# Loading q and k in longer rows, with the queries ordered by residue mod 8, in an attention and feed-forward kernel

## The chip, the core and the metric

The kernel runs on one core of one Trainium2 chip. A core has TensorE (PE: matmuls; its weight loads are listed apart as PEld), VectorE (DVE), ScalarE (ACT), GpSimd (POOL) and SyncE (SP, which here only issues transfers), and 16 DMA engines between HBM and the on-chip memory SBUF. TensorE writes into PSUM. The metric is the time of one execution on the device, in microseconds (us). Three runs of the kernel before took 181.08, 181.47 and 181.53 us, median 181.47.

## The reference

Two parts follow one another. The first is attention with 4 batches, 8 heads, 768 tokens and 64 numbers for each head. A query sees the 96 last tokens (itself included) and the first 8 tokens of the sequence, with a bias that grows linearly with distance. The second is a feed-forward layer on 3,072 tokens of width 512, inner width 1,024.

```python
scores = np.matmul(q, k.transpose(0, 1, 3, 2)) / np.sqrt(D)
is_global = pos[None, :] < n_global                      # 8
is_local = (rel >= 0) & (rel < n_local)                  # 96
keep = is_global | is_local
dist = np.where(is_global & ~is_local, float(n_local), np.abs(rel))
scores = np.where(keep, scores - slopes[:, None, None] * dist[None], -1e9)
a = softmax(scores)
x = np.matmul(a, v)            # then heads side by side: [3072, 512]

h = x @ w_in                   # [3072, 1024]
solu = h * softmax(h)
ln = (solu - mean) / np.sqrt(var + 1e-6) * g_ln
out = ln @ w_out               # [3072, 512]
```

Inputs and output are float32.

## The kernel before

The work is cut into 12 units: one unit is a batch and a third of its tokens (256 queries), for all 8 heads, numbered 0 to 11. What is done for a unit is a set of short steps, and a long string `ORDER` says in which order the steps are written into the program. Every engine and every queue works through its own instructions in just that order; waits between engines follow from the data. A step's name is followed by what it needs: an engine or queue (S for SP, A for ACT, D for DVE, P for POOL), the unit, and a head pair or a half.

```python
ORDER = """
gb id off:1 cap off:0 g:A dist:1 mask:1:0 dist:0 q:S:0 cq:A:0 tq:0 eq:A:0 zero k:S:0 ck:D:0 tk:0
ek:A:0 S:0:3 gk:0 mask:1:6 X:0:3 S:0:0 X:0:0 gS:0 mask:0:7 gX:0 v:A:0:0 mask:1:7 mask:0:2 mask:0:6
q:S:1 cq:D:1 k:S:1 mask:0:5 mask:0:1 S:0:1 S:0:2 X:0:1 tq:1 eq:A:1 ck:P:1 selV tk:1 ek:D:1 S:1:0
k:S:3 X:0:2 mask:0:3 ck:D:3 tk:3 q:S:2 v:S:0:1 ek:A:3 gk:1 fill cq:D:2 cv:D:0 gv0:0 q:S:4 q:S:3
... (cut)
o:A:9:1 d:S:10:1 O:10:1 o:A:10:1 Q:11:0:1 t:11:0:0 e:D:11:0:0 t:11:0:1 e:D:11:0:1 st:S:7 t:11:1:0
e:D:11:1:0 t:11:1:1 e:A:11:1:1 O:11:0:0 O:11:0:1 st:S:10 O:11:1:0 O:11:1:1 st:S:9 Z:P:11:0:1
o:D:11:0:0 o:D:11:0:1 st:S:11:0:1 Q:11:1:0 Q:11:1:1 Z:P:11:1:1 o:A:11:1:1 o:D:11:1:0 st:S:11:0:0
st:S:11:1:0 st:A:11:1:1
"""
```

The names: `q`, `k`, `v` load; `cq`, `ck`, `cv` cast to fp16; `tq`, `tk` turn q or k (64 numbers of a head onto partitions) on TensorE and `eq`, `ek` bring the result from PSUM to SBUF; `dq` turns q with a DMA transpose instead. `S` makes the scores of a head pair, `X` their exponentials, `M` multiplies them with the mask; `gS`, `gX` the same for the 8 global tokens; `L` the sums of the softmax, `I` their inverse, `V` the values, `N` the normalized result. For each half of a unit (128 tokens) `A` is the first product of the feed-forward layer, `E` its exponential, `U` the product of the two, `Q` its squares, `Z` the statistics, `d` a DMA transpose (`t` and `e` on TensorE for the last unit), `O` the second product, `o` its scaling, `st` the store. `wi`, `wo`, `g`, `sc`, `pr`, `sm`, `mean`, `ce`, `cm` load and prepare the weights. `warm:n` issues n matmuls on zeros.

The loads, the casts and the turning of q and k:

```python
    def staged(shape, name):
        return stage.tile(shape, FP32, name=name, tag="in32", bufs=NIN)

    def load_qk(queue, name, u):
        b, s = units[u]
        t = held[name + "32", u] = staged([P, H, 2 * D], name + "32")
        queues[queue].dma_start(
            out=t,
            in_=(q if name == "q" else k)[b, :, ts(s, UQ)].rearrange("h (p r) d -> p h (r d)", r=2),
        )

    def load_v(queue, u, j):
        b, s = units[u]
        if ("v32", u) not in held:
            held["v32", u] = staged([P, H, 2, D], "v32")
        queues[queue].dma_start(
            out=held["v32", u][:, :, j], in_=v[b, :, ts(2 * s + j, P)].rearrange("h p d -> p h d")
        )

... (cut)

    def warm_up(n):

        t = small([P, 512], FP32, "warm")
        for _ in range(n):
            nc.tensor.matmul(out=t, lhsT=held["zeros"][:, 0:P], rhs=held["zeros"],
                             start=True, stop=True)

... (cut)

    def cast_qk(engine, name, u):
        t = held[name + "16", u] = attn.tile([P, 2, H, D], FP16, name=name + "16")
        cast(engine, t, held.pop((name + "32", u)).rearrange("p h (r d) -> p r h d", r=2))

... (cut)

    def turn(name, u):
        src = held.pop((name + "16", u))
        t = held["p" + name, u] = small([P, 2, NPAIR, P], FP16, name + "turned")
        for r in range(2):
            for g in range(NPAIR):
                nc.tensor.transpose(
                    out=t[:, r, g, :],
                    in_=src[:, r, 2 * g : 2 * g + 2].rearrange("p h d -> p (h d)"),
                    identity=held["ident"],
                )

    def evac_q(engine, u):
        t = held["qT", u] = attn.tile([P, 2, NPAIR, QC], FP16, name="qT")
        cast(engine, t, held.pop(("pq", u)))

    def evac_k(engine, u):
        t = held["kT", u] = attn.tile([P, NPAIR, UQ], FP16, name="kT", bufs=4)
        cast(engine, t.rearrange("p g (i r) -> p g i r", r=2),
             held.pop(("pk", u)).rearrange("p r g i -> p g i r"))

    def turn_q_dma(queue, u):
        t = held["qT", u] = attn.tile([P, 2, NPAIR, QC], FP16, name="qT")
        queues[queue].dma_start_transpose(
            out=t.rearrange("p r g i -> p (r g) i"),
            in_=held.pop(("q16", u)).rearrange("p r h d -> p (r h d)"),
        )
```

In HBM a head's tokens lie one after another, 64 float32 numbers (256 bytes) each. `load_qk` puts tokens 2p and 2p+1 of all 8 heads on partition p: 128 partitions, 8 heads, runs of 512 bytes. The queries are then ordered with the even tokens first and the odd ones behind (r is 0 or 1), and so are the columns of scores, sums and values. Scores and norm read and write them like this:

```python
    def scores(u, g):
        s = units[u][1]
        qT = held["qT", u]
        sc = held["sc", u, g] = big("sc")
        for j, a, e, o in blocks(s)[0]:
            for m in range(2):
                r = slice(m * D, m * D + D)
                nc.tensor.matmul(
                    out=sc[:, m, o : o + e - a].rearrange("p (r i) -> p r i", r=2),
                    lhsT=held["kT", u - s + j // 2][r, g, ts(j % 2, P)],
                    rhs=qT[r, :, g, a // 2 : e // 2], start=True, stop=True,
                )

... (cut: expo, keep, the global tokens, sums, invert, values)

    def norm(u):
        xT = held["xT", u] = attn.tile([P, NPAIR, UQ], FP16, name="xT", bufs=3)
        nc.vector.tensor_tensor(
            out=xT, in0=held.pop(("pa", u)).rearrange("p g r i -> p g (r i)"),
            in1=held.pop(("rlb", u)), op=ALU.mult,
        )

... (cut: the feed-forward steps)

    def ff_turn_dma(queue, t):
        held["uT", t] = msb.tile([P, NFC, P], FP16, name="uT", bufs=3)
        queues[queue].dma_start_transpose(out=held["uT", t], in_=held["un", t])

... (cut)

    def store(queue, u, r=None, h=None):
        b, s = units[u]
        rows = out[ds(b * S + s * UQ, UQ), :].rearrange("(p r) c -> p r c", r=2)
        sl = slice(0, 2) if r is None else slice(r, r + 1)
        c = part(h, D_MODEL)
        queues[queue].dma_start(out=rows[:, sl, c], in_=held["osb", u][:, sl, c])
```

The store writes pairs of tokens again (r=2), 4 KB for each partition.

## Time and profile before

The profile is of one execution with a span of 182.2 us.

| | before |
|---|---|
| median of three runs | 181.47 us |
| span of the profiled execution | 182.2 us |
| mean granted TensorE clock | 0.981 of full |
| HBM read, written | 23.07 MB, 6.29 MB |
| loads of q, and of k | 12 of 512 KB each, median 6.6 and 7.1 us from issue to landing |
| loads of v | 24 of 256 KB |
| DMA transposes | 9 of q, 22 in the feed-forward layer |
| turning on TensorE (k: 96 matmuls, q: 24) | 9.5 and 3.1 us busy |

How to read it: a busy share is taken over the whole span. The page also cuts the span into 40 equal slices and gives the busy share of each in tenths (9 is 90% or more), for the engines and for the mean of the 16 DMA engines, and what they moved in GB/s. A list of waits says which engine, at which instruction, waited for which releaser: us in total, times, the longest. A stretch of time can be asked for by itself: then each engine's busy us (and instructions), the granted clock, the DMA share and GB/s follow. A packet is one contiguous piece that a DMA engine moves.

### The profile page before, as it was taken

Reading aid. Unit: us, or ns where it says so; the run is one execution under the profiler, and the core shown is the slowest. Engines: PE = TensorE matmul, PEld = TensorE weight load, DVE = VectorE, ACT = ScalarE, POOL = GpSimd, SP = SyncE. Lnnn points to the kernel's source line nnn. Section 1 sums busy time; section 2 is a strip of 40 time slices with the busy share of each in tenths; the row PEclk is TensorE's granted clock in tenths of the full one; section 3 lists DMA queues with packets and bytes.
Section 4 is the critical chain, followed back from the end, with each engine's and each line's share of the span. In section 5 each row is a group of like instructions: output and inputs, shape, how many; then the busy total and the mean of one; then the engine's idle time right before and its main releaser. Section 6 shows DMA issues by size and latency. Waiting matters only on the chain. (4 is left out here: it accounts for less than half of the span.)

```text
span 182.2 us, 3846 instructions
## 1 busy us (share of the span) xinstructions
PE 151.0 (83%) x1456; PEld 81.2 (45%) x1456; DVE 114.4 (63%) x180; ACT 144.1 (79%) x232; POOL 85.1 (47%) x188
## 2 busy tenths in 40 slices
PE   0474538995699499889999999999999999998880
...
DMA  5999999999899949799999999999979942068062
GB/s 117 279 290 252 271 205 177 280 306 243 191 294 234 159 114 167 150 258 155 200 294 290 147 157 274 182 251 277 281 93 323 246 89 58 4 140 262 13 242 90
DMA packets 87506, 36.69 MB, mean 201 GB/s; under 512 B 59456, under 2 KB 84544, under 8 KB 87488
## 3 DMA queue, kind: packets, MB, share of 16 engines
q1 hardware_dynamic: 83680, 34.74, 87.9%
q0 software_dynamic: 544, 1.05, 3.3%
...
q14 instruction: 7, 0.06, 0.1%
HBM read 23.07 MB, written 6.29 MB: 161 GB/s over the span
## 5 line engine op out<-in xcount | busy, mean ns | idle before, releaser
L344 ACT ACTIVATE pt<-sc 128x896 f16<-128x896 f32 (+1 forms) x48 | 40.0, 864 | 9.6 <-PE sc L335 9.3
L459 PE MATMUL ph<-w_in,xT 128*128 128x512 f16 x192 | 44.9, 380 | 1.2 <-DVE xT L444 0.7
L535 PE MATMUL po<-gw,uT 128*128 128x512 f16 x192 | 44.6, 379 | 0.3 <-DVE osb L547 0.2
L481 DVE SCALAR_TENSOR_TENSOR un<-e,ph 128x1024 f16<-128x1024 f16 (+1 forms) x26 | 29.2, 1135 | 15.9 <-ACT e L473 7.0
L351 DVE TENSOR_TENSOR pt<-pt,mask 128x896 f16<-128x896 f16 (+1 forms) x48 | 31.5, 685 | 4.4 <-ACT pt L344 4.3
L473 ACT ACTIVATE e<-ph 128x1024 f16<-128x1024 f32 (+1 forms) x26 | 24.8, 954 | 5.5 <-PE ph L459 4.8
L535 PEld LDWEIGHTS <-uT 128*128 128x128 f16 x192 | 18.2, 98 | 22.1 <-issue 0.7
L490 ACT ACTIVATE sq<-un 128x1024 f16<-128x1024 f16 (+1 forms) x26 | 25.7, 988 | 2.8 <-DVE un L481 2.6
L459 PEld LDWEIGHTS <-xT 128*128 128x128 f16 x192 | 17.5, 98 | 23.1 <-DVE xT L444 1.7
L444 DVE TENSOR_TENSOR xT<-pa,rlb 128x1024 f16<-128x1024 f32 x12 | 14.6, 1220 | 20.0 <-ACT rlb L416 16.8
L335 PE MATMUL sc<-qT,kT 64*128 64x128 f16 (+2 forms) x256 | 17.8, 260 | 5.6 <-ACT qT L135 2.5
L139 POOL CAST v<-v 128x1024 f16<-128x1024 f32 x9 | 9.7, 1084 | 20.7 <-DMA v<-in_v_dram 20.6
L335 PEld LDWEIGHTS <-kT 64*128 64x128 f16 x256 | 9.8, 105 | 14.2 <-issue 10.2
L510 POOL TENSOR_SCALAR w<-s,w 128x1 f32<-128x1 f32 x22 | 7.6, 344 | 17.6 <-ACT sq L490 11.9
L137 DVE COPY kT<-kturned 128x1024 f16<-128x1024 f16 x10 | 12.2, 1219 | 4.7 <-PE kturned L300 4.7
L398 PE MATMUL lb<-pt,ones 128*64 128x128 f16 (+2 forms) x256 | 11.3, 238 | 4.6 <-DVE un L481 3.8
L512 POOL TENSOR_TENSOR rs<-w,neghalf 128x1 f32<-128x1 f32 x24 | 13.7, 572 | 2.0
L427 PE MATMUL pa<-pt,v 128*64 128x128 f16 (+2 forms) x256 | 12.6, 251 | 1.9 <-DVE v L137 1.9
L549 ACT ACTIVATE osb<-po,rs 128x512 f32<-128x512 f32 (+1 forms) x13 | 8.6, 670 | 5.8 <-PE po L535 3.1
L416 ACT ACTIVATE rlb<-rlb 128x1024 f32<-128x1024 f32 x12 | 12.7, 1057 | 0.4
L547 DVE TENSOR_SCALAR osb<-po,rs 128x512 f32<-128x512 f32 (+1 forms) x13 | 8.7, 684 | 6.6 <-POOL both L501 2.3
L414 ACT ACTIVATE rlb<-lb 128x1024 f32<-128x1024 f32 x12 | 12.3, 1029 | 0.6 <-PE lb L406 0.6
...
## 6 DMA issues: line engine op xcount, KB each, us to landing
...
```

What stands on the lines that cost most here:

```text
L335: nc.tensor.matmul(out=sc[:, m, o : o + e - a].rearrange("p (r i) -> p r i", r=2), lhsT=held["kT", u - s + j // 2][r, g, ts(j % 2, P)], rh ...
L344: nc.scalar.activation(out=pt[:, :, 0:w], in_=held.pop(("sc", u, g))[:, :, 0:w], func=AF.Exp, scale=inv_sqrt_d)
L351: nc.vector.tensor_tensor(out=pt[:, :, 0:w], in0=pt[:, :, 0:w], in1=held["mask"][:, g, :, o : o + w], op=ALU.mult)
L416: nc.scalar.activation(out=rlb, in_=rlb, func=AF.Exp, scale=-1.0)
L427: nc.tensor.matmul(out=po[m * D : m * D + D, g, :, a // 2 : e // 2], lhsT=held["v16", u - s + j // 2][:, 2 * g + m, j % 2], rhs=pt[:, m, o ...
L444: nc.vector.tensor_tensor(out=xT, in0=held.pop(("pa", u)).rearrange("p g r i -> p g (r i)"), in1=held.pop(("rlb", u)), op=ALU.mult,)
L459: nc.tensor.matmul(out=held["ph", t][:, ts(fh, 512)], lhsT=held["xT", t[0]][:, j, ts(t[1], P)], rhs=held["w_in"][:, j, ts(fh, 512)], start ...
L473: nc.scalar.activation(out=held["e", t][:, f], in_=held["ph", t][:, f], func=AF.Exp, accum_out=s0)
L481: nc.vector.scalar_tensor_tensor(out=held["un", t][:, f], in0=held["e", t][:, f], scalar=1.0, in1=held["ph", t][:, f], op0=ALU.mult, op1=A ...
L490: nc.scalar.activation(out=sq[:, f], in_=held["un", t][:, f], func=AF.Square, accum_out=s2)
L512: eng.tensor_tensor(out=rs, in0=w3, in1=held["neghalf"], op=ALU.pow)
L535: nc.tensor.matmul(out=held["po", t], lhsT=held["uT", t][:, c, :], rhs=held["gw"][:, c, :], start=(c == 0), stop=(c == NFC - 1),)
```

## The change

q and k are loaded with 8 tokens for each partition instead of 2. The 256 tokens of a head then take 32 partitions, so the 128 partitions are filled by 4 heads: partition 32g + p holds tokens 8p to 8p+7 of heads 2g and 2g+1, as two runs of 2 KB. Each of the two heads of a pair is a load of its own (m is 0 or 1), 256 KB. It is meant to move the same bytes in fewer, longer packets. The queries are ordered by their residue mod 8 from there on; the norm writes them back into the order that the stores need. q of every unit is turned on TensorE, and the order of all steps was searched anew. In the new order 37 of the 48 halves of q and k are issued from SP and 11 from POOL; of the 24 loads of v 9 are issued from POOL. Evacuations of q are 11 on DVE and 1 on ACT (3 on ACT before, 9 turned by DMA), and there are 35 matmuls on zeros (12 before), 18 of them at the very end. Cut from the diff: the end of the orders, and the same change of 2 to NR in the queries' offsets, the global tokens, the sums and the values.

```diff
@@ -17,56 +17,61 @@
 P = 128
 UQ = 256
+NR = 8
 FAR = 30000.0
 
 NIN, NV = 13, 4
 
 ORDER = """
-gb id off:1 cap off:0 g:A dist:1 mask:1:0 dist:0 q:S:0 cq:A:0 tq:0 eq:A:0 zero k:S:0 ck:D:0 tk:0
-ek:A:0 S:0:3 gk:0 mask:1:6 X:0:3 S:0:0 X:0:0 gS:0 mask:0:7 gX:0 v:A:0:0 mask:1:7 mask:0:2 mask:0:6
... (the other old lines are cut)
-st:S:11:1:0 st:A:11:1:1
+cap gb off:0 dist:0 g:A off:1 dist:1 k:S:0:0 q:S:0:0 k:S:0:1 mask:0:7 mask:1:0 mask:0:0 id selV
+fill ck:D:0 tk:0 ek:D:0 mask:0:5 mask:0:3 q:S:0:1 cq:A:0 q:S:1:0 q:S:2:0 k:S:1:0 k:S:1:1 zero
+k:P:2:0 k:P:2:1 gk:0 q:S:1:1 tq:0 q:P:3:0 k:S:3:0 k:S:3:1 v:S:0:0 v:A:0:1 hm eq:D:0 S:0:3 gS:0
+S:0:1 ck:D:1 tk:1 cq:D:1 ek:D:1 cv:P:0 mask:1:6 mask:1:3 mask:0:6 S:0:0 q:S:2:1 tq:1 eq:D:1 gS:1
+S:1:1 mask:0:2 mask:1:5 mask:0:4 mask:1:4 gv0:0 ck:A:2 gX:0 mask:0:1 k:S:4:0 q:S:3:1 k:S:6:0
+q:S:4:0 q:P:4:1 k:S:4:1 X:0:0 X:0:3 X:0:1 k:S:6:1 v:S:1:0 v:S:1:1 M:0:0 ck:D:3 gX:1 tk:2 S:1:0
+mask:1:2 S:0:2 X:1:1 S:1:2 k:S:8:0 cq:D:2 tq:2 ek:D:2 k:S:8:1 k:S:5:0 k:P:5:1 wi:0 eq:D:2 q:S:5:0
+q:S:5:1 mask:1:1 mask:1:7 X:0:2 X:1:0 X:1:2 M:1:2 gv:0 S:2:0 X:2:0 wo:S:6 M:0:2 S:2:1 S:1:3 X:2:1
+S:2:2 v:S:2:0 ck:P:6 M:1:0 wo:S:0 q:S:6:0 gS:2 gX:2 ck:P:4 M:0:3 M:0:1 X:2:2 X:1:3 wi:2 warm:5:3
+cq:P:4 tk:3 ek:A:3 cv:P:1 gk:1 S:2:3 X:2:3 v:P:2:1 cq:D:3 M:2:1 tq:3 M:2:0 L:0 I:0 cq:P:5 eq:D:3
+M:1:3 S:3:3 X:3:3 V:0 M:1:1 S:3:2 v:S:3:0 X:3:2 tk:4 ek:A:4 wo:S:4 wo:A:2 L:1 N:0 I:1 S:3:1
+q:P:6:1 X:3:1 tq:4 eq:D:4 M:3:3 V:1 M:3:2 N:1 S:4:0 v:P:3:1 tk:6 X:4:0 ek:D:6 S:4:2 ck:P:8 X:4:2
+ck:A:5 k:S:7:0 sc:P:0 k:S:9:0 sc:P:3 q:S:7:0 q:S:7:1 v:S:4:0 S:4:3 gS:3 gX:3 X:4:3 S:4:1 X:4:1
+A:1:0 E:1:0 M:4:2 M:2:3 M:3:1 M:2:2 M:4:3 tk:5 ek:D:5 U:1:0 M:4:1 sc:A:7 A:0:0 E:0:0 sc:A:6 U:0:0
+d:S:0:0 cv:D:2 A:0:1 E:0:1 U:0:1 L:2 I:2 M:4:0 gS:4 tq:5 Q:0:0 gX:4 V:2 N:2 S:3:0 sc:A:2 A:1:1
+E:1:1 X:3:0 gk:2 eq:D:5 A:2:0 E:2:0 sc:D:1 tk:8 cq:D:6 tq:6 S:5:0 eq:A:6 X:5:0 A:2:1 U:1:1 cv:P:3
+gv0:1 k:P:7:1 ek:D:8 U:2:0 sc:P:4 M:3:0 gv:1 gS:5 sc:A:5 E:2:1 S:6:0 X:6:0 Q:0:1 L:3 I:3 gX:5
+d:S:1:0 mean k:S:9:1 L:4 q:S:10:0 v:S:5:0 U:2:1 V:3 cm I:4 v:P:4:1 v:S:6:0 pr:7 pr:5 Z:P:0:0 S:5:3
+warm:12 S:6:2 X:5:3 S:5:2 X:6:2 X:5:2 ce:0 N:3 ce:1 ce:2 ck:D:7 ce:3 ce:4 cq:P:7 cv:P:4 V:4
+v:S:6:1 N:4 S:5:1 S:6:1 Q:2:0 tk:7 X:6:1 M:5:2 ek:D:7 M:6:1 M:5:3 X:5:1 Q:1:0 Q:2:1 tq:7 ck:D:9
+eq:D:7 sm:5 pr:6 sm:6 A:3:0 E:3:0 Q:1:1 sm:7 O:0:0 o:D:0:0 Z:P:1:0 q:S:8:0 q:S:8:1 cv:P:6 gv0:2
+A:4:0 E:4:0 M:5:0 U:3:0 M:6:2 S:7:1 X:7:1 O:1:0 o:A:1:0 U:4:0 gv:2 S:6:3 X:6:3 S:7:3 X:7:3 S:7:2
+v:S:9:0 k:S:11:0 k:S:11:1 k:S:10:0 X:7:2 v:S:5:1 tk:9 S:7:0 X:7:0 gS:7 gX:7 M:5:1 L:5 I:5 M:6:0
+Z:P:1:1 M:6:3 A:4:1 E:4:1 ek:D:9 M:7:1 cq:P:8 v:P:9:1 k:P:10:1 A:3:1 tq:8 gS:6 M:7:0 cv:D:5 V:5
+q:P:11:0 Q:3:0 gX:6 U:4:1 Z:P:0:1 eq:D:8 d:S:0:1 v:P:7:0 Z:P:3:0 v:P:8:0 Q:4:0 v:P:7:1 d:S:3:0
+E:3:1 U:3:1 N:5 d:S:1:1 q:S:10:1 L:6 I:6 O:3:0 o:A:3:0 Q:3:1 M:7:3 M:7:2 ck:P:10 d:S:2:0 O:0:1
+o:A:0:1 v:S:10:0 d:S:2:1 st:S:0 Z:P:4:0 Z:P:2:1 cq:P:10 q:P:11:1 v:P:11:0 V:6 Z:P:2:0 cv:P:7
+v:S:10:1 S:8:3 X:8:3 S:8:1 X:8:1 O:1:1 o:A:1:1 S:8:0 X:8:0 L:7 S:8:2 st:S:1 I:7 gS:8 gX:8 X:8:2
+cq:P:11 d:S:4:0 q:S:9:0 N:6 ck:D:11 tq:10 A:5:1 E:5:1 eq:D:10 M:8:1 M:8:3 A:6:1 E:6:1 tk:10 U:5:1
... (cut)
+O:11:0:1 o:D:11:0:0 o:A:11:0:1 t:11:1:0 e:D:11:1:0 Q:11:1:1 Q:11:1:0 Z:P:11:1:1 t:11:1:1
+e:D:11:1:1 st:S:11:0:0 Q:9:1 st:S:11:0:1 O:10:1 Z:P:9:1 o:D:10:1 st:S:10 O:11:1:0 O:11:1:1
+o:D:11:1:1 st:S:11:1:1 o:D:11:1:0 st:A:11:1:0 O:9:1 o:A:9:1 st:S:9 warm:4:4 warm:5:2 warm:5:1
+warm:4:5
 """

... (cut)
@@ -95,8 +100,8 @@
     NPAIR = H // 2
     NU = S // UQ
     HD = H * D
-    QC = UQ // 2
-    assert NL % 2 == 0 and NL < P and NG % 2 == 0 and 2 * NG <= 32 and H == 8
+    QC = UQ // NR
+    assert NL % NR == 0 and NL < P and NG % NR == 0 and 2 * NG <= 32 and H * QC == 2 * P
 
     slopes = [float(2.0 ** (-8.0 * (h + 1) / H)) for h in range(H)]
     inv_sqrt_d = 1.0 / math.sqrt(D)

... (cut)
@@ -144,13 +149,14 @@
     def staged(shape, name):
         return stage.tile(shape, FP32, name=name, tag="in32", bufs=NIN)
 
-    def load_qk(queue, name, u):
+    def load_qk(queue, name, u, m):
         b, s = units[u]
-        t = held[name + "32", u] = staged([P, H, 2 * D], name + "32")
-        queues[queue].dma_start(
-            out=t,
-            in_=(q if name == "q" else k)[b, :, ts(s, UQ)].rearrange("h (p r) d -> p h (r d)", r=2),
-        )
+
+        if (name + "32", u) not in held:
+            held[name + "32", u] = staged([P, 2, NR * D], name + "32")
+        src = (q if name == "q" else k)[b, :, ts(s, UQ)].rearrange(
+            "(g m) (p r) d -> m g p (r d)", m=2, r=NR)
+        queues[queue].dma_start(out=held[name + "32", u][:, m], in_=src[m])
 
     def load_v(queue, u, j):
         b, s = units[u]

... (cut)
@@ -285,8 +291,8 @@
 
 
     def cast_qk(engine, name, u):
-        t = held[name + "16", u] = attn.tile([P, 2, H, D], FP16, name=name + "16")
-        cast(engine, t, held.pop((name + "32", u)).rearrange("p h (r d) -> p r h d", r=2))
+        t = held[name + "16", u] = attn.tile([P, NR, 2, D], FP16, name=name + "16")
+        cast(engine, t, held.pop((name + "32", u)).rearrange("p m (r d) -> p r m d", r=NR))
 
     def cast_v(engine, u):
         t = held["v16", u] = attn.tile([P, H, 2, D], FP16, name="v16", bufs=NV)

... (cut)
@@ -294,29 +300,27 @@
 
     def turn(name, u):
         src = held.pop((name + "16", u))
-        t = held["p" + name, u] = small([P, 2, NPAIR, P], FP16, name + "turned")
-        for r in range(2):
-            for g in range(NPAIR):
-                nc.tensor.transpose(
-                    out=t[:, r, g, :],
-                    in_=src[:, r, 2 * g : 2 * g + 2].rearrange("p h d -> p (h d)"),
-                    identity=held["ident"],
-                )
+        t = held["p" + name, u] = small([P, NR, NPAIR, QC], FP16, name + "turned")
+        for r in range(NR):
+            nc.tensor.transpose(
+                out=t[:, r].rearrange("p g i -> p (g i)"),
+                in_=src[:, r].rearrange("p m d -> p (m d)"), identity=held["ident"],
+            )
 
     def evac_q(engine, u):
-        t = held["qT", u] = attn.tile([P, 2, NPAIR, QC], FP16, name="qT")
+        t = held["qT", u] = attn.tile([P, NR, NPAIR, QC], FP16, name="qT")
         cast(engine, t, held.pop(("pq", u)))
 
     def evac_k(engine, u):
         t = held["kT", u] = attn.tile([P, NPAIR, UQ], FP16, name="kT", bufs=4)
-        cast(engine, t.rearrange("p g (i r) -> p g i r", r=2),
+        cast(engine, t.rearrange("p g (i r) -> p g i r", r=NR),
              held.pop(("pk", u)).rearrange("p r g i -> p g i r"))
 
     def turn_q_dma(queue, u):
-        t = held["qT", u] = attn.tile([P, 2, NPAIR, QC], FP16, name="qT")
+        t = held["qT", u] = attn.tile([P, NR, NPAIR, QC], FP16, name="qT")
         queues[queue].dma_start_transpose(
-            out=t.rearrange("p r g i -> p (r g) i"),
-            in_=held.pop(("q16", u)).rearrange("p r h d -> p (r h d)"),
+            out=t.rearrange("p r g i -> p r (g i)"),
+            in_=held.pop(("q16", u)).rearrange("p r m d -> p (r m d)"),
         )
 
     def pick_global_k(b):

... (cut)
@@ -333,9 +337,9 @@
             for m in range(2):
                 r = slice(m * D, m * D + D)
                 nc.tensor.matmul(
-                    out=sc[:, m, o : o + e - a].rearrange("p (r i) -> p r i", r=2),
+                    out=sc[:, m, o : o + e - a].rearrange("p (r i) -> p r i", r=NR),
                     lhsT=held["kT", u - s + j // 2][r, g, ts(j % 2, P)],
-                    rhs=qT[r, :, g, a // 2 : e // 2], start=True, stop=True,
+                    rhs=qT[r, :, g, a // NR : e // NR], start=True, stop=True,
                 )
 
     def expo(u, g):

... (cut)
@@ -442,8 +446,10 @@
     def norm(u):
         xT = held["xT", u] = attn.tile([P, NPAIR, UQ], FP16, name="xT", bufs=3)
         nc.vector.tensor_tensor(
-            out=xT, in0=held.pop(("pa", u)).rearrange("p g r i -> p g (r i)"),
-            in1=held.pop(("rlb", u)), op=ALU.mult,
+            out=xT.rearrange("p g (a i c) -> p g c a i", a=2, c=NR // 2),
+            in0=held.pop(("pa", u)).rearrange("p g (c a) i -> p g c a i", a=2),
+            in1=held.pop(("rlb", u)).rearrange("p g (c a i) -> p g c a i", a=2, c=NR // 2),
+            op=ALU.mult,
         )
```

## The prediction, made before the changed kernel had run

> **What bounds the kernel now.** I read the page's shares first, then its 40 slices, then the DMA queues, the waits, and last the busy time of two long stretches and of single windows.
>
> ```profile
> PE 151.0 (83%) x1456; PEld 81.2 (45%) x1456; DVE 114.4 (63%) x180; ACT 144.1 (79%) x232; POOL 85.1 (47%) x188
> PE   0474538995699499889999999999999999998880
> DMA  5999999999899949799999999999979942068062
> DMA packets 87506, 36.69 MB, mean 201 GB/s; under 512 B 59456, under 2 KB 84544, under 8 KB 87488
> q1 hardware_dynamic: 83680, 34.74, 87.9%
> ```
>
> No engine is full over the span, and the slices show why: TensorE (PE) has holes up to slice 18 and hardly one after it, while the 16 DMA engines are full up to slice 30. So two things bound the kernel in turn: transfers first, TensorE later. The packet line says why 36.69 MB fill the DMA engines: 59,456 of 87,506 packets are under 512 bytes, and the q and k loads (24 of 512 KB in 512 B runs, 24,576 packets) are most of the rest.
>
> ```profile
> 80.00:170.00 90.00, 88.42 (x849) 45.62 (x846) 58.55 (x90) 77.47 (x128) 48.77 (x112) 1.00 0.93 194
> 0.00:80.00 80.00, 56.59 (x574) 32.60 (x574) 53.28 (x85) 62.55 (x95) 32.26 (x63) 0.96 1.04 220
> ...
> POOL v L139 <- DMA v<-in_v_dram: 20.6, 3, 7.3
> ...
> POOL k L139 <- DMA k<-in_k_dram: 11.9, 4, 9.8
> ```
>
> The first two lines are the stretches (PE, weight load, DVE, ACT, POOL, clock, DMA share, GB/s): PE is busy 88.4 of 90 us from 80 to 170, but only 56.6 of the first 80, where DMA stands at 1.04 (packets overlap, so it can pass 1). The two waits show POOL's casts standing behind v and k loads. About 23 us of PE idleness in the first 80 us is what better transfers could win.
>
> **What the Trainium skill says.** Four places of "DMA: Bandwidth & Descriptors" bear on it.
> (1) "Why small descriptors are slow (HBM only)": each packet carries a fixed overhead. The trace agrees: a k load alone (84 to 90 us) moves 288 GB/s, 18 GB/s for each engine or 28 ns for 512 B, and 256 B packets of a lone transpose (152 to 157 us) move 223 GB/s, 18.4 ns each.
> (2) "Where 436 GB/s comes from": sixteen ports give 435.2 GB/s. The trace agrees for 4 KB packets:
>
> ```profile
> GB/s 437 437 410 355 437 437 137 0 0 0 0 0 24 188 220 218 217 195 213 200 249 460 411 382 382 410 437 437 410 191 0 0 0 0 0 0 0 0 0 0
> ```
>
> This is 164 to 170 us, where stores run: 437 GB/s is 27.3 GB/s for one engine.
> (3) "Why a DMA increments its semaphore by 16 and not by 1", under how many engines: the transfer is split along the slowest dimension (not of size 1) of both access patterns, over the largest number up to 16 that divides both sizes; on the SP and ACT queues these are the lowest-numbered engines, and from GpSimd (k below 16) consecutive ones from a moving cursor. In the kernel before every transfer I looked at has its 128 partitions outermost, so 16 engines; no run here shows a smaller number yet.
> (4) "Issuing engines are not separate DMA queues": another issuing queue brings no bandwidth. That is for judging the loads moved to GpSimd; the trace before has only w_in there.
>
> **The change, part by part.** *Loads.* A unit's q or k is now two loads of 256 KB, each 128 packets of 2 KB instead of 512 packets of 512 B. On 16 engines at 27.3 GB/s the 24 tensors would need 12.6 MB / 437 GB/s = 29 us in place of 24 x 64 packets x 28.4 ns = 44 us: 15 us saved. But the source of a half is walked as 4 head pairs (outermost), 32 rows, 512 numbers: the heads' stride does not merge with the rows'. By place (3) the split is then over the largest number dividing 4 and 128, which is 4. **I take this as what happens.** A half then puts 32 packets of 2 KB, 64 KB, on each of engines 0 to 3: 64 KB / 27.3 GB/s = 2.4 us, and nothing on the other twelve.
>
> *Load on engines 0 to 3, read down the new order as far as the second half of q of unit 10* (the place that proves tightest; both k halves of unit 10 need no more): 36 halves of q and k on SP, 36 x 2.4 = 86.4; 9 on GpSimd, a quarter of the time on these engines, 9 x 0.6 = 5.4; 19 loads of v, 64 packets of 18.4 ns each, 19 x 1.2 = 22.8; four of w_out (32 KB for each engine) 4 x 1.2 = 4.8; two of w_in (64 KB read) 2 x 2.4 = 4.8; five transposes of 66 packets, 5 x 1.2 = 6.0. Sum 130.2 us. The queue starts to move bytes at 2.0 us in the trace before, and about 2 us pass from the last byte to the semaphore (a lone transpose lands after 3.0 us, of which 1.2 are packets). So that half lands near 134 us if engines 0 to 3 never idle.
>
> *TensorE after that place.* The new order turns q of unit 10 only then, and TensorE works in order. Behind it stand (each from its row of the groups before: union busy time by its count): 14 of the 24 first products, 44.9/24 = 1.87 each, 26.2; 19 of 24 second products, 44.6/24 = 1.86, 35.3; 12 score steps, 17.8/48 = 0.37, 4.5; 4 sums, (11.3+4.0)/12, 5.1; 5 values, (12.6+4.4)/12, 7.1; 3 global scores 0.8; 5 turns of 0.79 (9.5/12), 4.0; last transposes and a global value 1.9. Sum 84.9. At the end the last useful matmul of before stops 4.9 us ahead of the span's end (177.3 of 182.2), which I keep; the 18 zero matmuls added at the very end, 18 x 0.235 = 4.2 us, lie beside the last store. With 1.05 for the cast: 134 + 1 + 85 + 5 = **225 us**.
>
> The same sum at other places in the order gives 215 (unit 5: 65.4 us of transfers, 139 of TensorE), 215 (unit 7: 90.0 and 115), 218 (unit 8: 108.6 and 99), 205 (unit 9, turned last). That the places agree within 20 us says the bound does not hang on one of them. The sum may be 4 us too long: in 72 to 74 us v and a transpose together reach 272 to 292 GB/s, 15 ns for 256 B. I choose **221**.
>
> *q turned on TensorE.* Nine DMA transposes go (9 x 1.2 = 11 us for each DMA engine); nine turns of 0.79 come, +7.1 us of PE, and 9 more evacuations of q. With the engines chosen anew, DVE has 11 of 1.22 us, +13.4, and ACT two fewer. PE's total becomes about 151 + 7.1 + 23 warm matmuls x 0.235 (5.4) = 163.5; DVE about 126. Neither sets the end if the above holds.
>
> *Eight runs instead of two* in the queries' order changes the patterns that TensorE and VectorE walk (the norm writes with a step of 4). Counts and elements stay, so I take no cost. The start moves: four halves stand ahead of q of unit 0, so it lands at 2.0 + 4 x 2.4 + 2 = 13.6 us, where before q landed at 5.4 and k at 7.4.
>
> **The rivals.** *A: the loads run on 16 engines.* Then 15 + 11 = 26 us come off every DMA engine, and the new order reads as made for that: loads stand further apart and TensorE's queue is fuller between them. If half of the 23 us of holes close and 8 us of turns and warming are added, the time is 176 to 180. For it: an order searched anew ought to suit its kernel. Against it: the pattern has a 4 outermost, and a search is only as good as the transfer model it uses. I give it 0.19.
> *B: GpSimd becomes the wait.* Twenty loads move to its queue, at 0.85 us of issue each (w_in's two cost 1.70 us in the groups): +17 us on 85, far from full; but it works in order, and a load that waits for a staging buffer would hold back the statistics. Alone this makes 183 to 190.
> *C: TensorE alone.* With transfers no bound, 163.5 us of PE less the 4.2 at the end, 5 to 10 us of start and 5 of end give about 172; the kernel before shows 31 us of idle PE, so this is a floor rather than a forecast.
>
> **Range and chances.** With the split over four engines (0.81) I expect 221 with some 9 us either way: 2.4 us for a half is near its least, stalls of SP's queue would add, faster small packets would take off. Without it, 176 to 190. The range 203 to 240 leaves out nearly all of rival A and the far ends of the main case. Faster by over 2% (below 177.8): 0.13; within 2%: 0.06; slower by over 2% (above 185.1): 0.81.
>
> **What would show it.** Right: PE's share falls to some 73% with holes reaching past the middle of the span; the mean DMA share falls to 0.5 to 0.6 although q and k are waited for, since twelve engines stand half empty; packets fall by about 18,432 for q and k and 9,800 for the transposes, to near 59,000; a lone half of q or k takes over 4 us to land, and during the first 10 us only some 109 GB/s flow from SP; the largest waits are casts of q and k on DMA. Wrong: a lone half that lands within 3 us and moves 300 GB/s or more, which makes rival A true at once; or long waits on POOL's statistics with the DMA engines idle, which is rival B. If PE is busy 98% of the second half from 80 us on, as before, the bound of four engines was not there.

## The result, and the profile after

The changed kernel takes 260.7 us (260.1 to 261.1) against 181.5 (181.1 to 181.5) before: the ratio is 1.437, 95% interval 1.433 to 1.442. The direction and the cause were as predicted; 221 us was 40 too low, and outside the range. Executions fall into a faster and a slower state: times and ratios here are of the faster one, while the profiles of the kernel before and of experiments 10 and 14 show executions of the slower one, 1 to 2% longer.

The page after: busy shares, TensorE and DMA in 40 slices of 6.5 us, packets, SP's queue.

```profile
PE 164.3 (64%) x1551; PEld 89.2 (34%) x1551; DVE 128.7 (50%) x189; ACT 144.3 (56%) x231; POOL 100.6 (39%) x209
PE   0013044940340499897750039989999999998887
DMA  2325423725378873696537961599947664535444
DMA packets 52279, 34.36 MB, mean 133 GB/s; under 512 B 42788, under 2 KB 43300, under 8 KB 52260
q1 hardware_dynamic: 45508, 26.88, 47.3%
```

Before, the DMA row was full (9) up to slice 30 and TensorE had hardly a hole after slice 18. Now TensorE has holes up to slice 23, and the DMA row stands at 2 and 3 in many slices in which TensorE waits for data. A 2 is what four of sixteen engines give when they are full. The same stretch alone, from 17 to 20 us, while SP has only q and k under way:

```profile
DMA packets 148, 0.29 MB, mean 98 GB/s; under 512 B 4, under 2 KB 4, under 8 KB 148
q1 hardware_dynamic: 148, 0.29, 26.2%
```

98 GB/s at a share of 26% is four engines at 24.5 GB/s, not sixteen waiting: a packet took about 85 ns (an estimate: 0.262 x 16 engines x 3 us, by 148), and experiment 1 shows that it takes no longer there. The trace doesn't number the engines; "engines 0 to 3" is the prediction's name for these four. Some of the longest waits (us in total, times, longest) say who suffers:

```profile
POOL v L144 <- DMA v<-in_v_dram: 28.9, 4, 18.5
POOL k L144 <- DMA k<-in_k_dram: 21.7, 1, 21.7
DVE un L487 <- DMA uT<-un: 20.3, 1, 20.3
POOL q L144 <- DMA q<-in_q_dram: 16.6, 3, 14.9
```

Casts of q, k and v wait for loads. The third line is new in kind: VectorE waits 20 us for the buffer `un`, which a DMA transpose has yet to read. Where that stands is shown by the chain of work that ended last, in order of time (start, us, what; most lines left out):

```profile
...
67.46 17.24 DMA q<-in_q_dram
85.19 1.03 ACT rlb L418
...
120.11 7.84 DMA v<-in_v_dram
...
134.28 17.18 DMA uT<-un
151.59 1.24 DVE un L487 x2
...
172.87 0.55 PE qturned L305 x8
```

The run has four parts. To 85 us it is SP issuing loads, and loads landing. From 85 to 120 it is TensorE, ACT and DVE at work. From 120 to 152 it is a load of v (7.8 us) and a transpose (17.2 us), with 6 us of POOL between them. From 152.9 to the end at 258.4 it is mostly TensorE, once more with a load of v in it (7.0 us, from 184). The table of stretches (us, PE, weight load, DVE, ACT, POOL, clock, DMA share, GB/s) shows the third part as a standstill:

```profile
134.00:152.00 18.00, 0.00 (x0) 0.00 (x0) 0.41 (x1) 0.47 (x1) 6.83 (x13) 0.57 0.85 146
152.00:173.00 21.00, 19.43 (x232) 11.34 (x232) 15.42 (x20) 16.64 (x25) 10.39 (x18) 0.88 0.55 112
```

For 18 us TensorE issues nothing; the granted clock stands at 0.57 meanwhile. Right after it TensorE is nearly full (19.4 of 21 us).

### The profile page after: what moved, and what is told of

It reads as the page before. It is cut to its first block, busy times and chain, and to the rows that moved or that the text cites. A ratio compares the mean times of both kernels' runs of the same rounds, so it can differ in the third digit from the quotient of the medians.

```text
span 258.4 us, 4079 instructions
## 1 busy us (share of the span) xinstructions
PE 164.3 (64%) x1551; PEld 89.2 (34%) x1551; DVE 128.7 (50%) x189; ACT 144.3 (56%) x231; POOL 100.6 (39%) x209
## 2 busy tenths in 40 slices
DMA packets 52279, 34.36 MB, mean 133 GB/s; under 512 B 42788, under 2 KB 43300, under 8 KB 52260
## 4 chain that ended last, share of the span: by engine, by line
SPq 26%; PE 26%; DMA 19%; DVE 8%; ACT 8%; POOL 7%; issue 6%; POOLq 0%; ACTq 0%; DVEq 0%
SPq L159 22%; PE ph L465 9%; DMA q<-in_q_dram 7%; DMA uT<-un 7%; PE po L541 6%; DMA v<-in_v_dram 6%; DVE xT L448 5%; SPq L165 4%; PE lb L402 2%; ACT e L479 2%; PE sc L339 2%; PE pa L431 2%; ACT sq L496 1%; ACT rlb L420 1%; PE warm L236 1%
## 5 line engine op out<-in xcount | busy, mean ns | idle before, releaser
L465 PE MATMUL ph<-w_in,xT 128*128 128x512 f16 x192 | 46.8, 391 | 4.3 <-DVE xT L448 3.3
L487 DVE SCALAR_TENSOR_TENSOR un<-e,ph 128x1024 f16<-128x1024 f16 (+1 forms) x26 | 29.4, 1135 | 32.5 <-DMA uT<-un 20.3
L339 PE MATMUL sc<-qT,kT 64*128 64x224 f16 (+2 forms) x256 | 18.0, 263 | 36.9 <-DVE un L487 20.0
L448 DVE TENSOR_TENSOR xT<-pa,rlb 128x1024 f16<-128x1024 f32 x12 | 29.4, 2452 | 20.7 <-ACT rlb L420 17.7
L305 PE MATMUL kturned<-ident,k 128*128 128x128 f16 x96 | 10.8, 281 | 40.1 <-DVE k L142 26.0
L465 PEld LDWEIGHTS <-xT 128*128 128x128 f16 x192 | 18.3, 100 | 27.0 <-issue 6.2
L355 DVE TENSOR_TENSOR pt<-pt,mask 128x896 f16<-128x896 f16 (+1 forms) x48 | 27.2, 603 | 0.0
L541 PEld LDWEIGHTS <-uT 128*128 128x128 f16 x192 | 18.2, 98 | 21.6 <-issue 0.5
L305 PEld LDWEIGHTS <-k 128*128 128x128 f16 x96 | 8.6, 128 | 43.5 <-DVE k L142 26.5
L516 POOL TENSOR_SCALAR w<-s,w 128x1 f32<-128x1 f32 x22 | 8.4, 381 | 33.7 <-ACT sq L496 32.1
L418 ACT ACTIVATE rlb<-lb 128x1024 f32<-128x1024 f32 x12 | 12.3, 1026 | 16.3 <-DMA q<-in_q_dram 14.4
L142 DVE COPY qT<-qturned 128x1024 f16<-128x1024 f16 x11 | 7.6, 695 | 19.0 <-PE qturned L305 18.9
L142 DVE CAST k<-k 128x1024 f16<-128x1024 f32 x6 | 4.8, 806 | 21.7 <-DMA k<-in_k_dram 21.7
L144 POOL CAST q<-q 128x1024 f16<-128x1024 f32 x7 | 7.3, 1039 | 20.2 <-DMA q<-in_q_dram 16.6
L553 DVE TENSOR_SCALAR osb<-po,rs 128x512 f32<-128x512 f32 (+1 forms) x13 | 8.8, 686 | 11.8 <-POOL rs L518 6.4
```

Of the source, the lines that this page charges most:

```text
L144: nc.gpsimd.tensor_copy(out=out, in_=in_)
L305: nc.tensor.transpose(out=t[:, r].rearrange("p g i -> p (g i)"), in_=src[:, r].rearrange("p m d -> p (m d)"), identity=held["ident"],)
L339: nc.tensor.matmul(out=sc[:, m, o : o + e - a].rearrange("p (r i) -> p r i", r=NR), lhsT=held["kT", u - s + j // 2][r, g, ts(j % 2, P)], r ...
L355: nc.vector.tensor_tensor(out=pt[:, :, 0:w], in0=pt[:, :, 0:w], in1=held["mask"][:, g, :, o : o + w], op=ALU.mult)
L448: nc.vector.tensor_tensor(out=xT.rearrange("p g (a i c) -> p g c a i", a=2, c=NR // 2), in0=held.pop(("pa", u)).rearrange("p g (c a) i -> ...
L465: nc.tensor.matmul(out=held["ph", t][:, ts(fh, 512)], lhsT=held["xT", t[0]][:, j, ts(t[1], P)], rhs=held["w_in"][:, j, ts(fh, 512)], start ...
```

## The experiments

**1. The source's dimensions in another order, so that 32 rows are outermost instead of 4 head pairs.** The same bytes in the same 2 KB runs. A partition then holds head pair p mod 4 of row p div 4, so the evacuations sort out the head pairs.

```diff
-            "(g m) (p r) d -> m g p (r d)", m=2, r=NR)
+            "(g m) (p r) d -> m p g (r d)", m=2, r=NR)
...
-        cast(engine, t, held.pop(("pq", u)))
+        cast(engine, t, held.pop(("pq", u)).rearrange("p r i g -> p r g i"))
```

> The changed kernel with one thing undone: partition 4p + g instead of 32g + p, so that the source of a half is walked with its 32 rows outermost and not with its 4 head pairs; same packets of 2 KB, same order of steps, the evacuations sort the head pairs. Theory 1 (a half of q or k runs on four DMA engines, and these bound the kernel): a half runs on 16 engines, GB/s while q and k load alone rises from 98 to over 300, the time falls to 174 to 184 us. Theory 2 (the new order makes SP's queue wait for computing, and loads stand behind its waits): stays over 230 us. Theory 3 (the slower norm, 2.45 us instead of 1.22, and the slower clock): stays over 245 us.

190.3 us, ratio 1.049 (1.040 to 1.057). From 3 to 8 us, first after the change, then here:

```profile
DMA packets 722, 0.47 MB, mean 93 GB/s; under 512 B 515, under 2 KB 515, under 8 KB 722
```

```profile
DMA packets 874, 1.63 MB, mean 325 GB/s; under 512 B 143, under 2 KB 143, under 8 KB 874
```

A packet of SP's queue took about 87 ns here (an estimate: 751 packets at a share of 81.8% in these 5 us), much as the 85 ns after the change; only more of them run side by side. The dimension order takes 70 of the 79 us away, though q's evacuation pays for it (1.22 us instead of 0.69). 190.3 us is 6 above the 174 to 184 that were expected. That the split follows the outermost dimension, as the Trainium skill says ("DMA: Bandwidth & Descriptors", "Why a DMA increments its semaphore by 16 and not by 1"), is borne out by this pair. The runs below on sixteen engines all keep this edit.

**2. The norm reads with a step and writes contiguously.** Of the remaining 9 us. Its 12 operations take 2.45 us each after the change, 1.22 before.

```diff
-            out=xT.rearrange("p g (a i c) -> p g c a i", a=2, c=NR // 2),
+            out=xT.rearrange("p g (a i c) -> p g a i c", a=2, c=NR // 2),
```

(Both inputs are turned in the same way.)

> As e1, and the norm walks its output contiguously and its two inputs with strides, where the changed kernel walks the inputs in runs of 32 and writes with a step of 4 numbers. If the strided write in fp16 is what doubled the norm, it falls from 2.45 to about 1.3 us, 12 x 1.15 = 14 us of VectorE less, and the time by 0 to 4 us against e1. If the five-dimensional walk itself costs, it stays at 2.4 us and the time at e1's.

186.6 us, ratio 1.028 (1.019 to 1.036), 3.7 us below experiment 1. The groups of `xT` in the kernel before, after the change and here:

```profile
L444 DVE TENSOR_TENSOR xT<-pa,rlb 128x1024 f16<-128x1024 f32 x12 | 14.6, 1220 | 20.0 <-ACT rlb L416 16.8 <-PE pa L437 3.3
```

```profile
L448 DVE TENSOR_TENSOR xT<-pa,rlb 128x1024 f16<-128x1024 f32 x12 | 29.4, 2452 | 20.7 <-ACT rlb L420 17.7 <-PE pa L441 2.9
```

```profile
L448 DVE TENSOR_TENSOR xT<-pa,rlb 128x1024 f16<-128x1024 f32 x12 | 23.2, 1937 | 6.0 <-ACT rlb L420 3.4 <-PE pa L441 2.6
```

The same elements cost 1.22 us in order, 1.94 read with a step, 2.45 written with a step; 1.94 lies between the 1.3 and the 2.4 that were expected. The step is the price of the eight residues.

**3. The change with the step order of before** (and its DMA transposes of q).

```diff
-< the new ORDER >
+< the ORDER of before, loads by halves >
```

> The changed layout (head pairs outermost, halves of 2 KB packets) in the order of steps of the kernel before, with its nine DMA transposes of q. Theory 1: still on four engines, 215 to 260 us; all halves on SP are 48 x 2.67 = 128 us of engines 0 to 3 at 98 GB/s. Theory 2 (the new order is at fault): 180 to 195 us.

269.2 us in one run: the new order isn't at fault; it is some 8 us better than the old one on four engines.

**4. All q and k halves issued by GpSimd.**

```diff
-k:S:0:0 q:S:0:0 k:S:0:1 ... q:S:10:1
+k:P:0:0 q:P:0:0 k:P:0:1 ... q:P:10:1
```

> The changed kernel with all 48 halves of q and k issued from GpSimd instead of 11; still four engines for each. If the engines of a GpSimd load come from a moving cursor, the halves spread over all 16 and SP's queue is free for v, transposes and stores: 190 to 220 us although GpSimd gets 37 x 0.84 = 31 us more to do. If they stay on the same four engines: 245 us or more. Theory 2 expects a gain too, since loads no longer stand behind SP's waits, but with loads alone still at 98 GB/s; so the GB/s in the first 20 us tells the two apart.

238.5 us in one run. From 8 to 13 us it moves

```profile
DMA packets 862, 0.98 MB, mean 196 GB/s; under 512 B 624, under 2 KB 624, under 8 KB 862
q0 software_dynamic: 862, 0.98, 107.3%
```

Twice the 98 GB/s of SP's halves, with all sixteen engines full: halves from GpSimd do not all fall on the same four engines. The time lies between the two expectations. Sixteen full engines moved 325 GB/s in experiment 1 and move 196 here, so a half from GpSimd costs more engine time than one from SP; experiment 9 puts a number to it.

**5. Queries in token order, with TensorE doing the walk** (sixteen engines; masks, scores, values and norm in token order; a score's moving operand is read with a step of 128 numbers, which the texts put on record call 512, the weights of the first product with a step of two columns).

```diff
-                    rhs=qT[r, :, g, a // NR : e // NR], start=True, stop=True,
+                    rhs=qT[r, :, a // NR : e // NR, g].rearrange("p r i -> p i r"), start=True, stop=True,
```

> As e1 (rows outermost, 16 engines, the changed kernel's order of steps), but the queries stay in the order of the tokens: q is brought out of PSUM as it lies, and the moving operand of the score matmuls walks it by (token, residue), with strides of 4 and 512 numbers; everything behind is in token order, the norm is contiguous, and the first product of the feed-forward layer takes every second column of xT as its weights. If strides cost TensorE nothing, the score matmuls stay at 0.37 us a step, the norm returns from 2.45 to 1.22 us and the evacuation of q from 1.22 to 0.69 us: VectorE falls from 139.8 to about 119 us and the time from 190.3 to 177 to 184. If strided reads slow TensorE, score steps or weight loads grow and the time stays at 186 or more.

202.2 us, ratio 1.115 (1.109 to 1.120). The norm is back at 1.24 us, but the scores take the gain and more. In experiment 1 and here:

```profile
L339 PE MATMUL sc<-qT,kT 64*128 64x224 f16 x96 | 12.6, 275 | 3.3 <-DVE qT L142 3.3
```

```profile
L338 PE MATMUL sc<-qT,kT 64*128 64x224 f16 x96 | 26.7, 553 | 1.4 <-DVE qT L142 1.4
```

A moving operand of 224 columns takes 553 ns with the large step, 275 in runs of 28 consecutive numbers. The weights with a step of two cost nothing: a first product's matmul is 389 ns here, 387 there.

**6. The same with the old step order, q turned by TensorE right before its scores.**

```diff
-< the new ORDER >
+< the ORDER of before, dq:S:u replaced by tq:u eq:D:u >
```

> As e5, but in the order of steps of the kernel before; its nine DMA transposes of q are replaced by turns on TensorE set right before the first scores of the unit. If the new order is worth something by itself, e5 is faster than this by 2 us or more; if the order that was searched for a slower transfer path serves as well, both agree within 2 us. About 178 to 188 us.

234.9 us, ratio 1.294 (1.286 to 1.302). It mixes experiment 5's slow scores with turns on TensorE in an order that was made for DMA transposes, so it says only that the old order doesn't carry these turns as it is.

**7. The change with one DMA transpose of `un` issued earlier,** ahead of q of unit 8.

```diff
-Z:P:1:0 q:S:8:0 q:S:8:1 ... eq:D:8 d:S:0:1 v:P:7:0
+Z:P:1:0 d:S:0:1 q:S:8:0 q:S:8:1 ... eq:D:8 v:P:7:0
```

> The changed kernel with one issue moved: the DMA transpose of unit 0, second half, goes on SP's queue ahead of q of unit 8 instead of behind the k halves of units 11 and 10. If the standstill from 134 to 152 us comes from this transpose being held up behind loads on engines 0 to 3, the time falls by 8 to 18 us, to 241 to 251. If the standstill has another cause, or the next transpose is held up as long, it stays within 4 us of 258 to 261.

267.1 us in one run, 6 more than the change and outside both expectations. q of unit 8 is turned at 142.3 us, 18 earlier than after the change, but q of unit 10 at 171.8, only 1 earlier. The standstill has moved on to v:

```profile
157.43 0.69 DVE L141 CAST v<-v 128x1024 f16<-128x1024 f32 x1 [16.93 <-DMA v<-in_v_dram]
```

So that one transpose isn't the cause: with it out of the way, a load of v is waited for as long.

**8. Experiment 5 without the 18 zero matmuls at the very end.**

```diff
-st:S:9 warm:4:4 warm:5:2 warm:5:1 warm:4:5
+st:S:9
```

> As e5 without the 18 matmuls on zeros at the very end (they compute nothing that is used). If they lie beside the last store, as I took in the prediction, the time is e5's within 0.5 us; if TensorE's last zero matmul ends after the store, it is 0.5 to 1.5 us shorter.

201.8 us, ratio 1.112 (1.108 to 1.117): the same as experiment 5. The zero matmuls cost nothing that shows; they lie beside the last store.

**9. Loads alone.** A small kernel that computes nothing of the reference and stores zeros: 8 halves by SP (A), 8 by GpSimd (B), 6 of each together (C), a transpose alone, 6 halves by SP with a transpose behind them (E), and 8 halves with rows outermost (F), each phase after the one before has landed.

> Loads by themselves, nothing computed (zeros are stored as output), in phases that wait for one another: A, 8 halves of q from SP with the head pairs outermost; B, 8 such halves from GpSimd; C, 6 of k from SP and 6 from GpSimd together; T, one DMA transpose of a 128 x 1024 fp16 tile alone; E, 6 halves of k from SP and one transpose behind them on the same queue; F, 8 halves of q from SP with the rows outermost. If four engines carry a half: A moves 98 GB/s (2.67 us a half, 21 us), F over 320 GB/s (7 us). If GpSimd's halves rotate over all engines: B moves well over 98 GB/s and C more than A and B one after the other would; if they use engines 0 to 3 as well, B is 98 and C 98. Transpose: about 3 us alone; in E it lands only when the 6 halves are through engines 0 to 3, some 16 + 3 us.

Its timeline (start, us, what): the issues and the last landing of A, the last landing of B, the transpose alone, and the transpose of E, each with its landing; the other times told below are from the same view.

```profile
1.08 12.17 SPq L625 DMA_DIRECT2D A<-in_q_dram  x8
24.91 0.16 DVE L648 TENSOR_TENSOR token<-token,A 128x1 f32<-128x1 f32 x1 [2.24 <-DMA A<-in_q_dram]
...
41.98 0.16 DVE L648 TENSOR_TENSOR token<-token,B 128x1 f32<-128x1 f32 x1 [0.59 <-DMA B<-in_q_dram]
...
72.60 1.34 SPq L660 DMA_TRANSPOSE trx<-unx  x1
75.83 0.16 DVE L650 TENSOR_TENSOR token<-token,trx 128x1 f32<-128x1 f32 x1 [3.30 <-DMA trx<-unx]
...
83.30 7.39 SPq L660 DMA_TRANSPOSE trx<-unx  x1
95.53 0.16 DVE L650 TENSOR_TENSOR token<-token,trx 128x1 f32<-128x1 f32 x1 [0.71 <-DMA trx<-unx]
```

A: from the first landing (6.72 us, left out) to the eighth are 18.2 us for seven halves, so **a half takes 2.60 us**, and not 2.4. The eight issues take 12.2 us: when the last one is through, at 13.3 us, some three halves have landed (an estimate: 6.72 and 2.60 for each more), so SP ran about five ahead and then had to wait. B: 16.4 us for 8. C: 28.6 us for 6 and 6, no less than A's and B's rates one after the other (6 x 2.60 = 15.6, and 12.3). The transpose alone lands 3.2 us after its issue began; behind six halves it takes 12.2, of which 7.4 are SP standing in the issue. F: 9.6 us for 8 halves.

What a half costs the engines is in the queues' lines, first from 5 to 20 us (A), then from 30 to 40 us (B):

```profile
q1 hardware_dynamic: 765, 1.52, 26.3%
q0 software_dynamic: 1590, 1.69, 82.9%
```

A share of sixteen engines, times the stretch, by the MB moved, makes 10.9 us of engine time for a half from SP and 20.6 for one from GpSimd (estimates; a half is 0.262 MB). Spread evenly over sixteen engines the latter is 1.3 us on each.

**10. Token order by the evacuation of q.** Sixteen engines; q sorted into token order as k already is; scores, norm and masks in token order; TensorE and VectorE read contiguously.

```diff
-        t = held["qT", u] = attn.tile([P, NR, NPAIR, QC], FP16, name="qT")
-        cast(engine, t, held.pop(("pq", u)))
+        t = held["qT", u] = attn.tile([P, NPAIR, UQ], FP16, name="qT")
+        cast(engine, t.rearrange("p g (i r) -> p g i r", r=NR),
+             held.pop(("pq", u)).rearrange("p r i g -> p g i r"))
```

> As e1 (16 engines), with token order made once, where q is brought out of PSUM (as k is: 1.22 us instead of 0.69); the score matmuls read runs of consecutive numbers again, the norm is contiguous, xT's every second column serves as weights. VectorE: 139.8 - 14.7 (norm) = 125 us; TensorE as in e1, 158. If the norm's strides are what e1 loses against the kernel before, 181 to 186 us. If the new order or q's turn on TensorE is, 187 or more.

182.1 us, ratio 1.002 (0.997 to 1.007): as fast as before. The page:

```profile
PE 158.0 (87%) x1551; PEld 85.9 (47%) x1551; DVE 125.2 (69%) x189; ACT 143.6 (79%) x231; POOL 103.2 (57%) x209
DMA  5899999999999790086599951492993271944442
```

The DMA engines have holes from slice 13 on, and yet nothing is won: TensorE is idle 181.7 - 158.0 = 23.7 us instead of 31.2, 7.5 less, and has 7.0 us more to do.

**11. The change with one load for each head pair,** 32 partitions and 64 packets.

```diff
-        queues[queue].dma_start(out=held[name + "32", u][:, m], in_=src[m])
+        for g in (2 * m, 2 * m + 1):
+            queues[queue].dma_start(out=held[name + "32", u][32 * g : 32 * g + 32], in_=src[g])
```

> The changed kernel with nothing altered but the loads of q and k: each step issues two loads of 32 partitions (a head pair, 32 rows x 2 heads x 2 KB) instead of one of 128 partitions; layout, packets, order and evacuations stay. The rows stand outermost, so by the rule 16 engines. Theory 1: 182 to 192 us, by up to 4 us less than e1 where the evacuation of q had to sort (1.22 against 0.69 us); twice the issues may cost a part of it. If a load of 32 partitions does not spread over 16 engines: over 220.

203.5 us, ratio 1.119 (1.108 to 1.131). From 3 to 8 us it moves 241 GB/s, between 93 after the change and 325 in experiment 1: the loads leave the four engines but stay slower than experiment 1's, with twice the issues. The time lies between the two expectations. Why a load into 32 partitions is slower was not separated.

**12. Experiment 1 with q left unsorted:** a score's moving operand has a step of 4 numbers.

```diff
-                    rhs=qT[r, :, g, a // NR : e // NR], start=True, stop=True,
+                    rhs=qT[r, :, a // NR : e // NR, g], start=True, stop=True,
```

> As e1, but q comes out of PSUM as it lies (0.69 us), and the score matmuls walk it with a step of 4 numbers (8 bytes) along the tokens of a residue. In e5 the innermost step was 512 numbers and the score steps took 0.83 us instead of 0.36. If any step above 1 slows TensorE's moving operand, score steps stay near 0.8 us and the time over 198; if only long steps do, 0.36 to 0.45 us, VectorE 6 us less than e1, and 186 to 190.

193.1 us, ratio 1.056 (1.037 to 1.074), between the two expectations:

```profile
L339 PE MATMUL sc<-qT,kT 64*128 64x224 f16 x96 | 17.7, 371 | 4.6 <-DVE qT L142 4.6
```

371 ns lie between 275 (runs of consecutive numbers, experiment 1) and 553 (a step of 128, experiment 5). DVE's copy of q falls from 1.22 to 0.69 us, but TensorE pays more than DVE gains.

**13. The change with all loads on SP** (its 20 loads by GpSimd, 11 halves and 9 of v, at the same places of the order).

```diff
-k:P:2:0 k:P:2:1 ... v:P:7:0 Z:P:3:0 v:P:8:0 ...
+k:S:2:0 k:S:2:1 ... v:S:7:0 Z:P:3:0 v:S:8:0 ...
```

> The changed kernel with all 20 loads that GpSimd issues moved to SP at the same places of the order. The prediction counted a half issued by GpSimd as a quarter of an SP half on engines 0 to 3. If that was right, the 9 halves before the tight place now cost 9 x 2.0 us more and the time is 275 to 285. If a GpSimd half costs these engines as much as an SP half (the loads by themselves took as long together as one after the other), it stays at 255 to 265. If GpSimd's bursts are what holds the transposes up in the standstill at 134 to 152 us (four of its loads run from 135 to 148), it is 235 to 250.

273.0 us, 12 more than the change and 2 short of the 275 to 285 that the quarter gave, ratio 1.510 (1.493 to 1.528). The second half of q of unit 10 is issued at 166.7 instead of 152.3, 14.4 later; the prediction's quarter has 9 x (2.60 - 0.65) = 17.6, and the 1.3 us of experiment 9 would have 9 x (2.60 - 1.3) = 11.7. So a half from GpSimd costs engines 0 to 3 about 1.0 us (an estimate: 2.60 - 14.4/9; the loads of v that move along are in it): less than one from SP, which phase C of experiment 9 had left open, and more than the prediction's 0.6.

**14. The change with 21 of 22 transposes of `un` on TensorE,** shortly before the product that reads them, as the last unit already has it. (Where the DMA transposes stand, the steps would wait for one another in a circle, here and in experiment 16.)

```diff
-... d:S:0:1 ... O:0:1 ...
+... t:0:1:0 t:0:1:1 e:A:0:1:0 e:D:0:1:1 ... O:0:1 ...
```

> The changed kernel with 21 of its 22 DMA transposes of the second product's input (uT from un) made by TensorE, shortly before the product that reads them, and evacuated by ACT and DVE, as the last unit already has it; loads and the order of all else unchanged. SP's queue then holds loads and stores alone and never stands behind a transpose (it stood 11.8 us in two of them from 103 us and 18.0 us in three from 134 us). If the transposes in that queue are the term that was mis-sized, the stop of TensorE before the turn of q of unit 8 (20 us) shrinks to below 8, that turn comes at 135 to 148 instead of 160.7, and the time is 236 to 250, with some 17 us of turns added on TensorE (21 x 0.79), part of them in holes. If the transposes only waited for loads that take as long without them, the turn stays near 158 and the time is 258 to 275.

275.9 us; the profile is of a run of 281.7. That misses both times that were expected; experiment 15 says why. SP's queue, here and after the change:

```profile
131.87 6.46 SPq L164 DMA_DIRECT2D q<-in_q_dram  x1
```

```profile
134.28 17.97 SPq L535 DMA_TRANSPOSE uT<-un  x3
152.31 0.60 SPq L159 DMA_DIRECT2D q<-in_q_dram  x1
```

Without transposes in the queue the second half of q of unit 10 is out at 138.3 us, with them at 152.9: **five transposes cost the queue 14.6 us, not 6.** Standing in the issue is not the transposes' doing alone: with them gone, the loads that come next in the same two places stand there for 8.8 and 6.5 us. q of unit 8 is turned at 144.7, not 160.7, as expected, and no standstill of TensorE over 5 us is left between 86 and 180 us. But q of unit 10 is turned at 170.6, only 2.2 earlier: TensorE now has the new transposes ahead of it, and waits 4.1 us for one of their evacuations and 3.9 for a cast of v.

**15. The same on sixteen engines.** The edits of experiments 1 and 14 together.

```diff
-            "(g m) (p r) d -> m g p (r d)", m=2, r=NR)
+            "(g m) (p r) d -> m p g (r d)", m=2, r=NR)
```

> The same with rows outermost, so on 16 engines: the price of the 21 transposes on TensorE where transfers bound nothing. TensorE gets 17 us more; the time goes from 190 to 198 to 207. The difference from the run on four engines is then the whole of the split without transposes in the queue: 35 to 48 us if they were the mis-sized term, over 60 if not.

225.0 us, ratio 1.237 (1.223 to 1.251), 35 above experiment 1. On TensorE the transposes cost far more than their 17 us: TensorE has 175.7 us of work instead of 158.3, and is idle 222.9 - 175.7 = 47.2 us instead of 29.4. The second product now waits for the evacuations:

```profile
PE po L546 <- DVE uT L147: 7.7, 5, 4.1
```

So the time of experiment 14 is not to be read against the change but against this run: 275.9 - 225.0 = 51 us for the split over four engines, where the transposes in SP's queue make it 260.7 - 190.3 = 70. With the same compute order, some 20 us of the loss go with the transposes that stand behind the halves; 51 lies between the 35 to 48 and the 60 that were expected. The turn of q of unit 8 says the same: it comes 71.7 us later on four engines than on sixteen with the DMA transposes (160.7 and 89.0), 51.4 later without them (144.7 and 93.3).

**16. Both: all loads on SP, transposes on TensorE.**

```diff
-k:P:2:0 ... d:S:0:1 ...
+k:S:2:0 ... t:0:1:0 t:0:1:1 e:A:0:1:0 e:D:0:1:1 ...
```

> Both: all loads on SP and 21 transposes on TensorE, so that SP's queue is loads and stores alone. Moving GpSimd's loads to SP alone added 12 us. If transposes and GpSimd's loads are separate terms, this is 10 to 15 us above the run without transposes. If GpSimd's four loads at 135 to 148 us cost only because a transpose stood beside them, it is within 4 us of it.

283.9 us in one run, 8 and 2 above experiment 14's two: it decides nothing between the two expectations.

## Why the prediction was right in kind and short by 40 us

**Right: four engines.** A half moves at 98 GB/s, and the order of the dimensions is worth 70 us (experiment 1). All of it is lost ahead of the turn of q of unit 10, the place that the prediction chose; the chain above has that turn at 172.8 us. The turn of q of unit 5 after the change, then the turns of units 5 and 10 in experiment 1:

```profile
100.38 0.62 PE L305 MATMUL qturned<-ident,q 128*128 128x128 f16 x8
49.75 0.62 PE L305 MATMUL qturned<-ident,q 128*128 128x128 f16 x8
101.16 0.62 PE L305 MATMUL qturned<-ident,q 128*128 128x128 f16 x8
```

Unit 5 is 50.6 us apart, unit 10 is 71.6, and the ends of the spans are 70.7. So 51 us are lost by unit 5, and the other 21 come with the standstill (unit 7 is still 50.7 apart, unit 8 71.7).

Rival B plays no part: POOL waits 67 us for loads, its statistics wait 32.1 us for ACT, 20.0 of these in the standstill, and with all loads taken from POOL the kernel is slower (experiment 13). Nor does C: the same work of TensorE ends at 190 us once loads run on sixteen engines. That TensorE's total of 164.3 us is so near the 163.5 predicted is luck in part: the same matmuls take 158.3 in experiment 1, at a granted clock of 0.982 instead of 0.901. **Rival A was too hopeful** even where its condition holds: on sixteen engines 190, and 182 with scores and norm contiguous, not 176 to 180. The 7.5 us of holes that close are paid back as 7.0 us more of TensorE (experiment 10).

**The step that failed** is the sum for engines 0 to 3 with its ending: "that half lands near 134 us if engines 0 to 3 never idle", followed by one for the cast and 85 + 5 of TensorE, which made 225. Against that, q of unit 10 is turned at 172.8 instead of 135, 38 us late. Two terms of the sum were too small, and the overlap was wrong: TensorE was taken to be ready when the half lands. By terms:

- *A half:* 2.60 us instead of 2.4 (experiment 9; the trace after has 98 GB/s instead of 109). For 36 halves that is +7.2.
- *Five transposes:* 14.6 us instead of 6.0 (experiment 14), +8.6. I had counted the packets of a transpose; what it costs is its place in a queue that runs in order: it waits for the halves ahead of it (3.2 us alone, 12.2 behind six halves) and SP stands in its issue meanwhile. SP spent 11.8 and 18.0 us in the issue of the five, from 102.7 and 134.3 us on, about half of which a load in their place would have stood too (8.8 and 6.5 us, experiment 14).
- *The rest of the transfers:* the half is out at 152.9 and its packets end at 158.4, so it lands near 159 (an estimate). That is 25 late, of which 15.8 are in the two terms above. Of the other 9, 1.6 are the start (first bytes at 3.6 us instead of 2.0) and some 4 to 6 are nine halves from GpSimd at 1.0 to 1.3 us instead of 0.6 (estimates, experiments 13 and 9). The rest is not placed.
- *From landing to turn:* 14 us instead of 1. I had taken it that TensorE would have done all that stands ahead of that turn by then. It had not: from 134 to 152 it stood still, for the buffer that an unfinished transpose held, and then needed 152.9 to 172.8 for that work, nearly all of it busy. This is +13.
- *TensorE after that turn:* 85.6 us to the end instead of 85 + 5, -4.

The sum is 225 + 7.2 + 8.6 + 9 + 13 - 4 = 259, where the span measured is 258.4; that I took 221 rather than 225 did the rest, for the hope of cheaper small packets. As the landing is taken from the trace, this sum has to close; it shows where the time went, and not that each term is right. The place in the order was well chosen, the remainder behind it right within 4 us; what a single place can't hold is that transfers and TensorE bound the kernel in turn. The chain has them alternate: transfers to 85, compute to 120, transfers to 152, TensorE after. A sum of one resource up to one place, then of the other, is a lower bound, and I used it as a middle. That the same sum at five places agreed within 20 us was no support, since all five share its terms: at unit 5 its 65.4 us of transfers put the turn near 70 (with 2.0 us before the first byte, 2 to the semaphore and 1 for the cast), and it came at 100.4. There too both parts were late: POOL waits for that q until 87.7, 18 us after the sum's landing, and the turn follows 13 us later.

**Terms of less weight.** GpSimd's halves at a quarter, 0.6 us: too little, 1.0 to 1.3 (experiments 13 and 9). "Counts and elements stay, so I take no cost" for the norm: wrong, 12 x 1.23 = 14.8 us more of DVE, worth at least 3.7 us of time on sixteen engines (experiment 2). q's evacuation: 0.69 us, not 1.22, since it copies in order; DVE's total came out at 128.7 for 126. The start: q of unit 0 is cast at 18.9 us where I had it land at 13.6; first bytes at 3.6 instead of 2.0, and 2.60 for 2.4, explain 2.4 of that. The signs: PE's share is 64%, not 73, and packets are 52,279, not 59,000. Where SP issues all loads there are 59,380 (experiment 13), so the count of SP's packets was right; GpSimd's loads go in fewer and larger ones.

**What stays open.** Why GpSimd's six halves took some 13 us from SP's in phase C of experiment 9 (28.6 - 15.6), where an even spread has 6 x 1.3 = 8, and why they cost twice the engine time of SP's; why 32-partition loads reach 241 GB/s only; the few us of transfers above, and about half of the 18 by which the transfers ahead of unit 5 were late. A version that beats the kernel before was not found; the best, experiment 10, equals it.
